# Narrow value products for three more heads, and a projection ahead of the last value piece, in a one-core decode step

## The chip, the cores and the metric

The kernel runs on one core of one Trainium2 chip. A time is the device time of one execution in microseconds (us). A core has a matrix engine (TensorE, PE in the profile, with its weight loads listed as PEld), a vector engine (VectorE, DVE), a scalar engine (ScalarE, ACT), GpSimd (POOL) and SyncE (SP), which here issues nearly all transfers. Each engine works through its own instructions in order and waits on semaphores for the others.

## The reference

A transformer block step for one token and a batch of four: a modulated layer norm, attention of 32 query heads over a cache of 8 key-value heads with 4096 positions each, and then a modulated MLP-Mixer whose token axis has length one.

```
mod = (silu(c) @ w_mod).reshape(4, 6, 1, 512)      # sa, ca, ga, sb, cb, gb
h = layernorm(x) * (1 + ca) + sa
q = (h @ wq)                       # 32 heads of 128
p = softmax(q k^T * 128**-0.5)     # each of 8 cached heads serves 4 query heads
x = x + ga * ((p v) @ wo)
h = layernorm(x) * (1 + cb) + sb
u = gelu(layernorm(h) * w1 + b1)   # for each channel, 1792 values
x = x + gb * (u @ w2 + b2)
```

All is float32. The key and value caches are 134 MB together.

## The kernel before

The cache is worked through in 32 "heads", one for each pair of batch entry and key-value head: head i belongs to batch entry i // 8. Each head's keys and values, 2 MB each, come through a ring of three large SBUF tiles (`ring`, tag "kv"). The transfers are issued by SyncE. For heads 0 to 23 a loop carries the work; heads 24 to 31 and the Mixer of the last two batch entries follow an order written out by hand in the string `PLAN` (lines 627 to 636), whose steps are read from left to right and issue their instructions at once. So each engine's order is the order in which the steps stand in that string.

The steps of a head i, with the letters of the plan:

- `s` scores (L238), `S`, `m`, `X`, `b`, `B`: the maximum; `e` exponentials (L268), with their sums; `t` transposes of the probabilities in two halves (L275).
- `l` (sums, L279): adds the sums up over partitions with a constant matrix, `grp`, or `grpl` for head 31. `L` (scale, L284 to L290): the reciprocal, spread into a selection tile of 4 x 4 columns, or of 4 for head 31 (L287).
- `v` (values): probabilities times values. For heads 0 to 30, eight products of 512 columns (L301), in two steps `vi.0` and `vi.1`: each takes four groups of positions at once and makes a 512-column result of which only the matching quarter is of use. For head 31, 32 products of 128 columns (`values_last`, L309), in four steps of 16, 8, 4 and 4 products. Either form writes 32 rows in one of four row groups of the result (`pv`, or `pve`) in turn.
- `V` (copy_v, L315): the result from PSUM to SBUF, 512 or 128 columns. `a` (pick, L324): one product for each 128 columns, four or one, which picks and normalises. `A` (copy_o, L329): its 128 x 4 result to SBUF.
- `p` (project): head times output weights. For heads up to 29, four products of 512 columns (L337) into `pa`, which `P` (add_up, L353) adds to the accumulator of its batch entry. For heads 30 and 31, 16 products of 128 columns each (L342), accumulated in `pgx`.

Around the end there are also `y` (the accumulator of the last batch entry folded, L358, into `pc`), `E` (the residual of the other heads from `pc`, L362 and L363), `I` (that residual added to `pgx` by a product, L685), `Y` (which names the tile `pgx` and issues nothing), `x` (two expansions for the Mixer of batch entry 2, L431), `f` (a gate multiplied into a piece of the output weights, L567) and `zs` (the first statistics of the last batch entry, L370). From there the last entry's norm and Mixer follow.

The last transfers, in the order in which SyncE issues them: values of head 28, of head 29, of head 30 in two halves, of head 31 in pieces of 16, 8, 4 and 4 groups of positions, and 1 MB of modulation weights. All of them have been issued by 353.5 us.

Where a value piece or a tile is used, the framework lets the engine wait for the transfer or for the last reader of its buffer.

Of the kernel before, what the change touches and what calls it, by code (L numbers as in the profile page):

```python
# [8 lines left out]
F32 = mybir.dt.float32  # L9
# [6 lines left out]
B, D, HQ, HKV, SK, DH, F = 4, 512, 32, 8, 4096, 128, 1792  # L16
# [3 lines left out]
P = 128  # L20
NS = B * HKV
NSM = 3 * NF + 16 + 1

# [8 lines left out]
def adaln_decode(ctx: ExitStack, tc: tile.TileContext, small, x, wmod, wq, kk, kv, vv, wo, out):  # L34
# [7 lines left out]
    ps_s = ctx.enter_context(tc.tile_pool(name="ps_s", bufs=2, space=PSUM))  # L42
    ps_v = ctx.enter_context(tc.tile_pool(name="ps_v", bufs=1, space=PSUM))
# [3 lines left out]
    mm = nc.tensor.matmul  # L47
    dv = nc.vector

    neg1 = pad.tile([1, 96], F32, name="neg1")[:, 0:1]  # L50
    sm = cst.tile([P, NSM], F32, name="sm")
    xr = wk.tile([P, D], F32, name="xr", tag="yw", bufs=1)[0:B]
# [28 lines left out]
    grp = cst.tile([P, 16, REP, 2], F32, name="grp")  # L81
    dv.tensor_copy(grp, eight.unsqueeze(1).unsqueeze(3).to_broadcast([P, 16, REP, 2]))
    grp = grp.rearrange("p j r e -> p (j r e)")
    grpl = cst.tile([P, 4, REP, 8], F32, name="grpl")
    dv.tensor_copy(grpl, eight.unsqueeze(1).unsqueeze(3).to_broadcast([P, 4, REP, 8]))
    grpl = grpl.rearrange("p c r x -> p (c r x)")
# [86 lines left out]
    def slots():  # L173
        return ring.tile([P, 2, SK], F32, name="kv", tag="kv")
# [29 lines left out]
    def load_wm5():  # L204
        t = slots().rearrange("p s (k n) -> p (s k) n", n=D)
        nc.sync.dma_start(t[:, 0:4], wmod[2][:, 1])
        WM[5] = t[:, 0:4]
        return t[:, 4:6]

    def load_key(t, i):  # L210
        nc.sync.dma_start(t, kv[i - 2][:, 0])
        key(t, i)

    def load_v(t, i, cuts):
        value(t, i)
        src = (kv[i][:, 1] if i < NS - 2 else vv[i - NS + 2]).rearrange("p (j d) -> p j d", d=DH)
        for lo, hi in zip(cuts, cuts[1:]):
            nc.sync.dma_start(VT[i][:, lo:hi], src[:, lo:hi])
# [12 lines left out]
    S, M, PL, SEL = {}, {}, {}, {}  # L231
# [38 lines left out]
    def turn(i, halves=range(2)):  # L270

        S.pop(i, None)
        for n in halves:
            p = PL[i][0][:, n * 512:(n + 1) * 512]
            dv.transpose(p, p)  # L275

    def sums(i):
        pl = ps_m.tile([P, 1], F32, name="pl", tag="m")
        mm(pl, grp if i < NS - 1 else grpl, PL[i][1], start=True, stop=True)  # L279
        SEL[i] = pl  # L280

    def scale(i):
        rl = wk.tile([P, 1], F32, name="rl")
        dv.reciprocal(rl, SEL[i])  # L284
        if i == NS - 1:
            SEL[i] = wk.tile([P, 1, REP], F32, name="sel", bufs=4)
            dv.tensor_scalar(SEL[i][:, 0], eight, rl, None, op0=OP.mult)  # L287
            return
        sel = wk.tile([P, 4, REP], F32, name="sel", bufs=4)
        dv.tensor_scalar(sel, sel4, rl, None, op0=OP.mult)  # L290
        SEL[i] = sel

    PV, PA = {}, {}

    def values(i, ks):
        if ks[0] == 0:
            PV[i] = ps_v.tile([P, 4 * DH], F32, name="pv", tag="pv")
        pT = PL[i][0]
        for k in ks:
            q = k % 4  # L300
            mm(PV[i][32 * q:32 * q + 32, :], pT[:, 128 * k:128 * k + 128:4],  # L301
               VT[i][:, 4 * k:4 * k + 4, :].rearrange("p j d -> p (j d)"), start=(k < 4), stop=(k >= 4))

    def values_last(i, ks, pv):
        PV[i] = pv
        pT = PL[i][0].rearrange("p (k r) -> p k r", r=32)
        for k in ks:
            for c in range(4):
                mm(pv[32 * c:32 * c + 32, :], pT[:, k * 4 + c, :], VT[i][:, k * 4 + c, :],  # L309
                   start=(k == 0), stop=(k == 7))  # L310
# [20 lines left out]
    def project(i, pa=None):  # L331
        b, h = divmod(i, HKV)
        oT = OT.pop(i)
        if pa is None:
            pa = ps_m.tile([P, D], F32, name="pa", tag="m")
            for g in range(REP):
                mm(pa[32 * g:32 * g + 32, :], oT[:, g:g + 1].to_broadcast([P, 32]), wo_t[h][:, g, :],  # L337
                   start=True, stop=True)
        else:
            for g in range(REP):  # L340
                for c in range(4):
                    mm(pa[32 * c:32 * c + 32, :], oT[:, g:g + 1].to_broadcast([P, 32]),  # L342
                       wo_t[h][:, g, c * P:(c + 1) * P], start=(g == 0 and h == HKV - 2),
                       stop=(g == REP - 1 and h == HKV - 1))
        PA[i] = pa
# [9 lines left out]
    def fold_groups(pool, acc, tag):  # L355
        pc = pool.tile([P, P], F32, name="pc", tag=tag)
        for c in range(4):
            mm(pc[32 * c:32 * c + 32, :], first, acc[:, c * P:(c + 1) * P], start=True, stop=True)  # L358
        return pc

    def residual(x1, pc):
        dv.tensor_mul(x1, pc, prep[:, 1])  # L362
        dv.tensor_add(x1, x1, prep[:, 0])  # L363
# [4 lines left out]
    def stats(xin, b):  # L368
        st = wk.tile([P, 6], F32, name="st")
        dv.bn_stats(st, xin)  # L370
        sm_ = wk.tile([P, 4, 6], F32, name="stm")
        dv.tensor_mul(sm_, st.unsqueeze(1).to_broadcast([P, 4, 6]), ident.rearrange("p (c r) -> p c r", c=4)[:, :, 8 * b:8 * b + 1].to_broadcast([P, 4, 6]))
        return sm_
# [190 lines left out]
    def fold_gate(gate, es):  # L564
        for e in es:
            w = wo_t[HKV - 2 + e // REP][:, e % REP]
            dv.tensor_mul(w, w, gate)  # L567
# [7 lines left out]
    for step in (turn, sums, scale):  # L575
        step(0)
    mix = None
    for i in range(NS - HKV):
# [7 lines left out]
        if i:  # L586
            pick(i - 1)
            copy_o(i - 1)
        turn(i + 1)
        sums(i + 1)  # L590
        scale(i + 1)
        if i:
            project(i - 1)
# [29 lines left out]
    pve = pgx = pc = ep = spare = slot = None  # L623
    gates = list(range(2 * REP))
    cuts = {NS - 1: (0, 16, 24, 28, 32), NS - 2: (0, 16, 32)}
    last = [(0, 1, 2, 3), (4, 5), (6,), (7,)]
# [4 lines left out]
    LK30 t27.1 S29 P26 v27.0 m29 l27 g LK31 T t28.1 X29 LT t28.0 s30 L27 S30 b29 v27.1 B29 e29 l28 m30 V27  # L631
    c LV28 L28 a27 g X30 t29.1 t29.0 l29 L29 s31 A27 LV29 b30 p27 x v28.0 B30 S31 m31 e30 f P27 LT LV30 X31
    v28.1 b31 l30 B31 e31 LV31 V28 L30 c t30.1 a28 l31 L31 v29.0 t31.1 v29.1 A28 p28 t30.0 V29 a29 v30.0
    A29 LW f v30.1 P28 p29 g V30 t31.0 a30 x v31.0 v31.1 v31.2 P29 A30 Y y f v31.3 p30 E V31 a31 I A31 p31
    zs g zq zg T2 c zx c zm zq zb0 zc T3 zg zb1 zw0 zn zw1
    """
    TABLE = {"s": scores, "S": row_max, "m": turn_max, "X": col_max, "b": spread_max, "B": copy_max, "e": expo,
# [6 lines left out]
    for step in PLAN.split():  # L644
        op, k = step.rstrip("0123456789."), step.lstrip("abcdefghijklmnopqrstuvwxyzABCDEFGHIJKLMNOPQRSTUVWXYZ")
        i, q = (int(n) for n in (k + ".0").split(".")[:2]) if k else (0, 0)
        if op in TABLE:
            TABLE[op](i)
        elif op in MIX:
            MIX[op]()  # L650
        elif op == "t":
            turn(i, [q])
        elif op == "v":
            if i < NS - 1:
                values(i, range(4 * q, 4 * q + 4))
                continue
            if q == 0:
                pve = ps_s.tile([P, 8, P], F32, name="pve", tag="s")[:, 0]
            values_last(i, last[q], pve)
        elif op == "p":  # L660
            project(i, pgx[:, 4] if i >= NS - 2 else None)
        elif op == "LT":
            slot = slots()
        elif op == "LK":
            load_key(slot[:, i % 2], i)
        elif op == "LV":
            load_v(slot[:, i % 2], i, cuts.get(i, (0, 32)))
        elif op == "LW":
            spare = load_wm5()
        elif op == "x":  # L670
            mix.expand(spare if mix.n == 6 else None)
        elif op == "f":
            fold_gate(gate, gates[:1])
            del gates[:1]
        elif step == "T":
            nc.scalar.activation(tab, neg1, AF.Exp)
        elif op == "Y":
            pgx = ps_s.tile([P, 8, P], F32, name="pgx", tag="s")
        elif op == "y":
            pc = fold_groups(ps_m, ACC.pop(B - 1), "m")  # L680
        elif op == "E":
            ep = cst.tile([P, P], F32, name="ep")
            residual(ep, pc)
        elif op == "I":
            mm(pgx[:, 4], ident, ep, start=False, stop=False)  # L685
        elif step == "T2":
            nc.scalar.activation(tab, neg1, AF.Abs_reciprocal_sqrt)
        elif step == "T3":
            nc.scalar.activation(tab, neg1, AF.Gelu_apprx_tanh)
        elif op == "zs":  # L690
            row.st = stats(pgx[:, 4], B - 1)
        elif op == "zx":
            dv.tensor_copy(XK[:, B - 1], pgx[:, 4])
        elif op == "zw":
            modmm(pgx[:, 0], 5, (0,) if i == 0 else (1, 2, 3))
        elif op == "zb":
            if i == 0:
                py = ps_s.tile([P, 8, P], F32, name="py3", tag="s")
            row.spread(py[:, 4:], (2 * i, 2 * i + 1))
# [35 lines left out]
```

## Time and profile before

| | |
|---|---|
| median of 3 runs | 389.47 us (389.02 to 390.22) |
| profiled execution, span | 386.9 us |
| mean granted clock of TensorE | 0.877 |
| read from memory | 157.32 MB, 407 GB/s over the span |
| TensorE busy | 298.9 us (77%) |
| VectorE busy | 215.2 us (56%) |
| chain that ended last | transfers 54%, TensorE 28%, VectorE 16% |

The profiled execution's own time is given by its span alone, from its first to its last instruction; the median of the runs is 2.57 us above the span. In a row of the timeline stand the start, the length of the merged group, the engine, the line, the operation, what it writes and reads, how often, and in square brackets how long the engine was idle before it and what ended that. A product of float32 counts as two records. Lengths of groups of products include a drain at the end that overlaps with what follows.

### The profile page before, as it was taken

To read this page: it belongs to the slowest core of one execution; us is meant where nothing else is said; L and a number is where in the kernel's file an instruction comes from. 1 tells how busy PE (TensorE), PEld (TensorE's weight loads), DVE (VectorE), ACT (ScalarE), POOL (GpSimd) and SP (SyncE) were. 2 spreads that over 40 slices of the span, in tenths; PEclk is the share of its full clock that TensorE was granted. 3 is DMA by queue.
4 is the path that set the end of the run, shared out by engine and by line. 5 is a ranking of instruction groups with operands and counts; after the bars stand their busy time and mean duration, and the time that the engine had idled before them with its cause. 6 is when DMAs were issued, how large, how long until landed. Compare 5 with 4: busy or idle time off the path is not lost.

```text
span 386.9 us, 5714 instructions
## 1 busy us (share of the span) xinstructions
PE 298.9 (77%) x2416; PEld 122.4 (32%) x2416; DVE 215.2 (56%) x516; ACT 108.0 (28%) x132; POOL 0.7 (0%) x6
## 2 busy tenths in 40 slices
PE   0765575863966949979888859999988887999984
PEld 0111121231323313334222323443323342444562
DVE  0420351620542524676766644676875579788766
ACT  0101120110110110113567210213783104757356
POOL 0000000000000000000000000000000000000000
PEclk9998875986695775989999985978999998899999
DMA  8999999999999999999999999999999999999910
GB/s 329 430 434 434 415 451 430 410 449 432 418 447 434 430 434 432 434 432 434 426 434 429 434 429 434 434 432 434 425 434 432 434 429 434 422 427 423 404 46 3
DMA packets 7281, 157.70 MB, mean 408 GB/s; under 512 B 964, under 2 KB 980, under 8 KB 1368
## 3 DMA queue, kind: packets, MB, share of 16 engines
q1 hardware_dynamic: 7248, 157.33, 94.8%
q8 instruction: 19, 0.31, 0.3%
q14 instruction: 6, 0.05, 0.0%
q10 hardware_dynamic: 8, 0.00, 0.0%
HBM read 157.32 MB, written 0.01 MB: 407 GB/s over the span
## 4 chain that ended last, share of the span: by engine, by line
DMA 54%; PE 28%; DVE 16%; issue 1%; SPq 1%; ACTq 0%; DVEq 0%
DMA kv<-in_kv 47%; PE s L238 8%; PE pv L301 7%; DMA wq<-in_wq 6%; DVE m L243 3%; DVE p L275 3%; PE pt L324 2%; PE pa L337 2%; PE pb L258 2%; DVE uu L431 1%; DVE mx L252 1%; DVE acc L353 1%; PE qs L152 1%; PE phb L417 1%; PE pve L309 1%
## 5 line engine op out<-in xcount | busy, mean ns | idle before, releaser
L238 PE MATMUL s<-kv,QT 128*32 128x512 f32 x512 | 76.2, 715 | 35.6 <-DMA kv<-in_kv 32.6
L268 ACT ACTIVATE p<-s,nm 128x1024 f32<-128x1024 f32 x32 | 35.6, 1114 | 199.0 <-DVE nm L263 198.9
L243 DVE TENSOR_REDUCE m<-s 128x1 f32<-128x1024 f32 x32 | 39.2, 1224 | 76.1 <-PE s L238 76.0
L301 PE MATMUL pv<-kv,p 128*32 128x512 f32 x496 | 75.0, 684 | 0.4 <-DMA kv<-in_kv 0.4
L275 DVE STREAM_TRANSPOSE p<-p 128x512 f32<-128x512 f32 x64 | 41.9, 687 | 1.7 <-ACT p L268 1.7
L324 PEld LDWEIGHTS pt<-sel,po 128*128 128x128 f32 x250 | 33.6, 208 | 28.7 <-issue 15.6
L238 PEld LDWEIGHTS s<-kv,QT 128*32 128x32 f32 x512 | 16.3, 125 | 81.3 <-DMA kv<-in_kv 45.3
L337 PE MATMUL pa<-wo,oT 128*32 128x512 f32 x240 | 35.3, 663 | 4.3 <-DVE oT L329 4.2
L324 PE MATMUL pt<-sel,po 128*128 128x4 f32 x250 | 36.2, 268 | 1.4 <-DVE po L315 1.4
L315 DVE COPY po<-pv 128x512 f32<-128x512 f32 x31 | 21.4, 689 | 17.0 <-PE pv L301 17.0
L252 DVE TENSOR_REDUCE mx<-pm 1x128 f32<-1x512 f32 x32 | 21.4, 671 | 0.8 <-PE pm L247 0.7
L258 PEld LDWEIGHTS pb<-neg,mx 1*128 1x128 f32 x64 | 10.8, 210 | 32.9 <-DVE mx L252 31.1
L487 ACT ACTIVATE u<-u 128x1024 f32<-128x1024 f32 x20 | 20.4, 1052 | 2.7 <-DVE u L431 2.6
L431 DVE TENSOR_SCALAR u<-hb,wr,sm 128x512 f32<-128x512 f32 x40 | 19.9, 541 | 1.0 <-PE py L442 0.9
L353 DVE TENSOR_TENSOR acc<-acc,pa 128x512 f32<-128x512 f32 x26 | 17.7, 681 | 3.6 <-PE pa L337 3.6
L268 ACT ACT_TABLE_LOAD x11 | 14.1, 1283 | 19.0 <-DVE nm L263 18.9
L137 PE MATMUL s<-wm,sT 128*4 128x512 f32 x16 | 8.4, 684 | 12.2 <-DVE sT L123 12.2
L258 PE MATMUL pb<-neg,mx 1*128 1x1 f32 x64 | 13.5, 278 | 5.3 <-DVE mx L252 5.3
L487 ACT ACT_TABLE_LOAD x13 | 16.7, 1283 | 0.2
L247 PE MATMUL pm<-ident,m 128*1 128x128 f32 x32 | 9.1, 286 | 9.8 <-DVE rl L284 3.8
L301 PEld LDWEIGHTS pv<-kv,p 128*32 128x32 f32 x496 | 14.1, 146 | 8.1 <-issue 2.1
L247 PEld LDWEIGHTS pm<-ident,m 128*1 128x1 f32 x32 | 2.5, 80 | 39.1 <-DVE rl L284 21.0
(144 smaller groups left out, 212.3 us busy)
## 6 DMA issues: line engine op xcount, KB each, us to landing
kv<-in_kv SPq DMA_DIRECT2D x28, 4096.0 KB, 20.8
wq<-in_wq SPq DMA_DIRECT2D x2, 4096.0 KB
wo<-in_wo SPq DMA_DIRECT2D x4, 2048.0 KB
kv<-in_kv SPq DMA_DIRECT2D x4, 2048.0 KB, 18.5
wm<-in_wmod SPq DMA_DIRECT2D x2, 2048.0 KB
kv<-in_kk SPq DMA_DIRECT2D x1, 4096.0 KB
kv<-in_vv SPq DMA_DIRECT2D x3, 1024.0 KB
wm<-in_wmod SPq DMA_DIRECT2D x1, 1024.0 KB
```

Of the source, the lines that this page charges most:

```text
L238: mm(s[32 * c:32 * c + 32, n * 512:(n + 1) * 512], QT[:, b, h, :], KT[i][:, (n * 4 + c) * 512:(n * 4 + c + 1) * 512], start=True, stop=True)
L243: dv.tensor_reduce(M[i], S[i], axis=AX.X, op=OP.max)
L252: dv.tensor_reduce(mx, M[i].rearrange("o (c r) -> o r c", c=4).unsqueeze(1).to_broadcast([1, 4, 32, 4]), axis=AX.X, op=OP.max)
L258: mm(pb, M[i].rearrange("o c r -> o (c r)"), neg1, start=True, stop=True)
L268: nc.scalar.activation(p, S[i], AF.Exp, bias=M.pop(i), accum_out=l)
L275: dv.transpose(p, p)
L301: mm(PV[i][32 * q:32 * q + 32, :], pT[:, 128 * k:128 * k + 128:4], VT[i][:, 4 * k:4 * k + 4, :].rearrange("p j d -> p (j d)"), start=(k < ...
L324: mm(pt, po[:, c * DH:(c + 1) * DH], sel[:, c, :], start=(c == 0), stop=(c == n - 1))
L337: mm(pa[32 * g:32 * g + 32, :], oT[:, g:g + 1].to_broadcast([P, 32]), wo_t[h][:, g, :], start=True, stop=True)
L353: dv.tensor_add(ACC[b], ACC[b], pa)
L431: dv.tensor_scalar(u[:, e, :], hb, wr[:, j:j + 1], b1[:, j:j + 1], op0=OP.mult, op1=OP.add)
L487: nc.scalar.activation(u, u, AF.Gelu_apprx_tanh)
```

## The change

Four things change.

1. Heads 28 to 30 form their value products as head 31 does: 32 products of 128 columns in place of 8 of 512. `values_last` becomes `values_narrow`, which takes its result tile from the pool of `pv` unless one is given.
2. Their sums and scales take the forms of head 31 (`grpl`, 4 columns), and since the result has 128 columns, the copy out of PSUM has 128 columns and the pick is one product.
3. The small copy of head 30's pick (`A30`) stands ahead of the expansions `x` rather than behind the addition `P29`; `P29` in turn falls behind the expansions and the gate product `f`.
4. The projection of head 30 (`p30`) and the residual of the other heads (`E`) stand ahead of the last value piece (`v31.3`) rather than behind it.

```diff
+NARROW = NS - 4
...
-        mm(pl, grp if i < NS - 1 else grpl, PL[i][1], start=True, stop=True)
+        mm(pl, grp if i < NARROW else grpl, PL[i][1], start=True, stop=True)
...
-        if i == NS - 1:
+        if i >= NARROW:
             SEL[i] = wk.tile([P, 1, REP], F32, name="sel", bufs=4)
...
-    def values_last(i, ks, pv):
-        PV[i] = pv
+    def values_narrow(i, ks, pv=None):
+        if ks[0] == 0:
+            PV[i] = ps_v.tile([P, DH], F32, name="pvn", tag="pv") if pv is None else pv
+        pv = PV[i]
         pT = PL[i][0].rearrange("p (k r) -> p k r", r=32)
         for k in ks:
             for c in range(4):
...
-    A29 LW f v30.1 P28 p29 g V30 t31.0 a30 x v31.0 v31.1 v31.2 P29 A30 Y y f v31.3 p30 E V31 a31 I A31 p31
+    A29 LW f v30.1 P28 p29 g V30 t31.0 a30 A30 x f v31.0 v31.1 v31.2 P29 Y y p30 E v31.3 V31 a31 I A31 p31
...
-            if i < NS - 1:
+            if i < NARROW:
                 values(i, range(4 * q, 4 * q + 4))
-                continue
-            if q == 0:
-                pve = ps_s.tile([P, 8, P], F32, name="pve", tag="s")[:, 0]
-            values_last(i, last[q], pve)
+            elif i < NS - 1:
+                values_narrow(i, range(4 * q, 4 * q + 4))
+            else:
+                if q == 0:
+                    pve = ps_s.tile([P, 8, P], F32, name="pve", tag="s")[:, 0]
+                values_narrow(i, last[q], pve)
```

## The prediction

> **What bounds the kernel now.** I read the page first, then the chain that ended last over the final sixty microseconds, then the timeline of that stretch, then the stretches of two microseconds for the granted clock. From the page:
>
> ```profile
> span 386.9 us, 5714 instructions
> DMA 54%; PE 28%; DVE 16%; issue 1%; SPq 1%; ACTq 0%; DVEq 0%
> q8 instruction: 19, 0.31, 0.3%
> ```
>
> The chain is transfers over most of the span. Its last part, in order of time (start, length, what):
>
> ```profile
> 336.33 21.56 DMA kv<-in_kv
> ...
> 358.03 1.95 PE pv L301 x16
> 359.98 0.86 PE pa L337 x8
> 360.84 1.00 PE pt L324 x8
> 361.84 2.04 PE pv L301 x16
> 363.88 0.86 PE pa L337 x8
> 364.74 1.01 PE pt L324 x8
> 365.75 1.78 PE pve L309 x56
> 367.53 0.22 PE pc L358 x8
> 367.75 0.42 PE pve L309 x8
> 368.17 0.87 PE pgx L342 x32
> 369.04 0.31 PE pt L324 x2
> 369.35 0.33 PE pgx L685 x2
> 369.68 1.05 PE pgx L342 x32
> ...
> 370.76 0.31 DVE st L370
> ```
>
> From 358.03, when head 29's values have landed, the chain is put down to TensorE alone, about 12.7 us of it up to the statistics at 370.76. Read only that far, every microsecond taken from the value products and picks of heads 29 and 30 would shorten the kernel. The timeline of the same stretch says otherwise:
>
> ```profile
> 361.77 2.11 PE L301 MATMUL pv<-kv,p 128*32 128x512 f32 x16
> 362.79 0.21 PEld L301 LDWEIGHTS pv<-kv,p 128*32 128x32 f32 x8 [0.80 <-DMA kv<-in_vv]
> 363.95 0.69 DVE L315 COPY po<-pv 128x512 f32<-128x512 f32 x1 [0.71 <-PE pv L301]
> 364.56 0.70 DVE L275 STREAM_TRANSPOSE p<-p 128x512 f32<-128x512 f32 x1
> 364.70 0.97 PEld L324 LDWEIGHTS pt<-sel,po 128*128 128x128 f32 x8 [0.86 <-DVE po L315]
> 365.18 0.96 DVE L431 TENSOR_SCALAR kv<-hb,wr,sm 128x512 f32<-128x512 f32 x2
> 365.68 1.85 PE L309 MATMUL pve<-kv,p 128*32 128x128 f32 x56
> 366.06 0.68 DVE L353 TENSOR_TENSOR acc<-acc,pa 128x512 f32<-128x512 f32 x1
> 366.66 0.15 DVE L329 COPY oT<-pt 128x4 f32<-128x4 f32 x1
> 366.73 0.68 DVE L567 TENSOR_TENSOR wo<-wo,gate 128x512 f32<-128x512 f32 x1
> 367.10 0.16 PEld L309 LDWEIGHTS pve<-kv,p 128*32 128x32 f32 x8 [0.17 <-DMA kv<-in_vv]
> 367.35 0.40 PE L358 MATMUL pc<-acc,g 128*32 128x128 f32 x8
> 367.74 0.16 PEld L309 LDWEIGHTS pve<-kv,p 128*32 128x32 f32 x8 [0.26 <-DMA kv<-in_vv]
> 368.35 0.28 DVE L315 COPY po<-pve 128x128 f32<-128x128 f32 x1
> 368.97 0.39 PE L324 MATMUL pt<-sel,po 128*128 128x4 f32 x2
> 369.39 0.16 DVE L329 COPY oT<-pt 128x4 f32<-128x4 f32 x1 [0.76 <-PE pt L324]
> ```
>
> Weight loads wait for transfers at 362.79 (second half of head 30), at 367.10 (third piece of head 31) and at 367.74 (its fourth and last). TensorE keeps pace with the stream; it does not lag behind it. The last piece can't be multiplied before about 367.74, whatever is saved ahead of it. **What sets the end is the time from there**: head 30's projection 0.87, a pick at 368.97, head 31's projection, the statistics and the last Mixer.
>
> **Narrow products of heads 28 to 30.** Eight products of 512 columns become 32 of 128 per head; in the records each counts twice, so 16 become 64. Head 31 shows the price: 56 of them in 1.85 us with a small wait inside, and the 32 of a projection, of the same shape, in 0.87. Two such are 1.74 for 64. The wide form takes 1.95 for 16 with its drain of about 0.2, so 1.75 issued. I take no change. Bounds: 0.3 less per head (the sixteen at 361.77 took 2.11, its wait included) to 0.4 more (56 in 1.85 scaled to 64 is 2.11, against 1.75). Cover: the next piece's landing.
>
> The copy out of PSUM falls from 0.69 to 0.28, the pick from 8 records (about 1.0) to 2 (0.31 in the chain): per head 0.4 on VectorE and 0.7 on TensorE, some 1.1 in a row, three times. The scale's output of 4 columns rather than 16, and the other constant in the sums, I cost at nothing: both stand ahead of the landing for which their head's pick waits anyway, and without that cover a product of this size is a part of the copy's 0.28.
>
> None of the 3.3 us reaches the end. For head 28 the next product waits for head 29's landing at 358.03. For head 29 the chain arrives at head 30 some 1.1 us sooner, at about 360.7, and its second half still waits until 362.79. For head 30 it reaches head 31 about 1.1 sooner than 365.68, where the first piece isn't in: 1.05 MB after 362.79, at the 157.70 MB in 386.9 us of the whole (408 GB/s), is an estimated 365.4. The 0.3 that may be gained there ends at 367.10, where the third piece lands. TensorE then idles where it used to catch up.
>
> **The order around the last piece.** On VectorE head 30's small copy (A30) goes ahead of the two expansions, and its addition for head 29 (P29) behind the gate product. On TensorE head 30's projection goes ahead of the last value piece. No transfer is moved and none is issued by a moved step; SyncE's, ScalarE's and GpSimd's orders stay.
>
> Walk it from the rows. Second half of head 30 at 362.79 as before; copy at 363.95 for 0.28, transpose to about 364.9. Head 29's projection issues until about 364.6; the pick with 0.39 is through at 365.0. VectorE waits about 0.1 for it, copies at 365.05, and takes 0.07 to the next start (366.66 to 366.73), 0.88 for the expansions (365.18 to 366.06), 0.60 for the product (366.06 to 366.66, the same length): P29 runs from about 366.6 to 367.3, half a microsecond later than before. The fold (pc) reads it. TensorE gets to the fold at 367.35 anyway, because of the third piece. So the later addition costs 0 to 0.1; I take 0. It has no slack left.
>
> From there, before against after. **Before:** fold, last piece at 367.74, projection hidden over the copy, pick at 368.97, that is 1.23 after the last piece. **After:** fold 367.35 with 0.22, projection 367.57 with 0.87, last piece at 368.44 instead of 367.74, its end with 0.42 at 368.86, then copy with 0.07 and 0.28 to 369.21, and 0.06 to the pick (as 364.64 to 364.70): 369.27. The projection filled TensorE while the copy ran; now the copy stands bare, and the piece that had landed at 367.74 waits 0.7 behind the projection. The gap between the third and the last landing, 0.64, is too small for 0.22 of piece, 0.22 of fold and 0.87 of projection. Pick to head 31's projection and all behind it keep their lengths: the residual (E, I) is ready before, since its two VectorE steps of 0.29 follow the fold by 0.9.
>
> The sum: 369.27 - 368.97 = **+0.3 us**. The profile's one execution has a span of 386.9 us; the median of the runs is 389.47, 2.57 above it for what lies around the span, and I keep that difference: 389.47 + 0.3 = **389.8**.
>
> **The rivals.**
>
> *Faster: the last piece lands late enough.* The new order needs 0.83 from the last piece to the pick (0.42, 0.07, 0.28, 0.06) where the old one needs 1.23. If TensorE had finished the projection when the piece lands, 0.4 would be gained: 389.1. It decides where the landing comes later than 367.74 by 0.3 to 0.4. The 0.26 of waiting at 367.74 speaks for a late piece, the projection's 0.87 against it. Chance 0.16. Even then the gain is inside 0.3% (1.17 us), which is about what a measurement of this kernel can tell from no change.
>
> *Slower: the instruction transfers.* Three heads issue 48 records and as many weight loads more each, less 6 of each for the picks: 252 instructions. The 19 instruction packets carry 0.31 MB, 16 KB each; 0.3% of 16 engines' 386.9 us is 18.6 us, about 1 us for each, on one transfer engine. An added packet, if it falls on the engine that ends last, delays the last pieces by up to 1.0: the third piece at 368.1, the pick at 370.2, so 1.2 over before: 390.7. For it: the engines are all but full until the end. Against it: one of sixteen must be the late one. Chance 0.2 for 0.5 or more of it.
>
> *Slower: the granted clock.* TensorE now idles in several pieces between 360.5 and 367. The stretches (length, busy time of each engine, clock, DMA share) show what a long idle piece does:
>
> ```profile
> 324.00:326.00 2.00, 0.36 (x1) 0.08 (x1) 2.00 (x4) 0.00 (x0) 0.00 (x0) 0.88 1.03 442
> 328.00:330.00 2.00, 2.00 (x24) 0.79 (x16) 0.34 (x1) 1.99 (x3) 0.00 (x0) 0.50 0.99 426
> ```
>
> After 0.36 us of work in 2 the clock was 0.50 at 328. If that happened here, the 3.4 us of TensorE's work between the fold and the statistics would double: about 393. Against it: even with 2 us taken out of the nine from 358 to 367, TensorE is busy over 70% of the time there. Chance 0.05. [...]
>
> *Slower: narrow products that don't overlap.* The view of line 309 gives the weight loads alone:
>
> ```profile
> L309 PEld LDWEIGHTS pve<-kv,p x64: 106/110/110, 365.7 to 367.8; 128*32 128x32 f32 x64
> ```
>
> If each of the 64 cost its own 0.11, a head would take 7.0 in place of 1.75. Head 29 from 358.03 to 365.1, projection and pick 1.2, head 30 to 373.3, 1.2 again: head 31 at 374.5 in place of 365.7, so about 398. The 56 in 1.85, 0.033 each, speak against it. Chance 0.02. [...]
>
> *The change does not reach the end at all:* 389.5, between forecast and the faster rival, in the likeliest one's range.
>
> **How the numbers follow.** Forecast (with the no-effect case) 0.57, late landing 0.16, instruction packets 0.20, clock 0.05, narrow products 0.02. The likeliest's own range is 389.3 to 390.2, its 0.3 plus or minus the spread of the runs before (389.02 to 390.22, 0.6 either side). Taking in the late landing below and most of the packets above gives 389.0 to 390.8. Over 0.3% slower (above 390.64) are the clock, the narrow products, and under half of the packets' case, with some of the forecast's upper tail: 0.20. Over 0.3% faster needs more than the 0.4 that any order here can give; 0.06 is left for what I don't see. Within: 0.74.
>
> **What would show it.** In the profile after: head 31's first products at about 365.4 behind a wait for a transfer; waits for transfers at all four pieces but the last; the last piece's products right behind the projection with no wait, near 368.4; the copy of head 31 with TensorE idle beside it; the pick near 369.3; the three copies at 0.28 and picks at 0.3 to 0.4. Wrong would be: a last piece still waiting for its transfer behind the projection (the gain then is 0.4), landings later than 367.74 by most of a microsecond, a clock under 1 after 360, or 64 narrow products over 2.1 us.

## The result, and the profile after

The changed kernel takes 390.18 us (median; 389.65 to 391.54) against 389.44 us (388.85 to 390.64) for the kernel before, measured in turn on the same chip. The ratio is 1.0017, with a 95% interval of 1.0009 to 1.0025: 0.35 to 0.97 us more, inside the 0.3% that was called no change.

The traced executions differ by more (1.4 us) than the medians (0.74), and this goes with it: the runs of the kernel before fall into two groups, 12 of 21 up to 389.5 us and 9 from 389.8 us on, the profiled one has the span of the lower group, all runs of the changed kernel but one lie between 389.65 and 390.66, and what sets the upper group no trace shows.

From the page of the changed kernel:

```profile
span 388.3 us, 5965 instructions
DMA 54%; PE 26%; DVE 16%; ACT 2%; issue 1%; SPq 0%; DVEq 0%; ACTq 0%
q8 instruction: 20, 0.33, 0.3%
```

The span is 1.4 us longer, there are 251 instructions more, and one instruction packet more. This execution took 390.09 us, 1.8 above its span. The chain of the changed kernel (start, length, what):

```profile
348.78 18.70 DMA kv<-in_vv
367.52 1.05 PE pve L312 x24
368.56 0.22 PE pc L361 x8
368.78 0.87 PE pgx L345 x32
369.66 0.26 PE pve L312 x8
369.94 0.30 DVE po L318
370.29 0.39 PE pt L327 x2
370.67 0.33 PE pgx L690 x2
371.00 1.05 PE pgx L345 x32
372.08 0.31 DVE st L373
```

Before, this chain ran through TensorE from 358.03. Now one transfer holds it until 367.5, the second piece of head 31's values, and only then do the pieces, the fold, the projection (0.87) and the last piece (0.26) follow. The copy at 369.94 now stands in the chain, which it did not before. The timeline of the same stretch:

```profile
358.17 1.95 PE L312 MATMUL pvn<-kv,p 128*32 128x128 f32 x64 [0.41 <-DMA kv<-in_kv]
360.19 0.29 DVE L318 COPY po<-pvn 128x128 f32<-128x128 f32 x1 [0.68 <-PE pvn L312]
360.92 0.39 PE L327 MATMUL pt<-sel,po 128*128 128x4 f32 x2
362.94 1.08 PE L312 MATMUL pvn<-kv,p 128*32 128x128 f32 x32 [0.62 <-DMA kv<-in_vv]
365.23 0.16 DVE L332 COPY oT<-pt 128x4 f32<-128x4 f32 x1 [0.23 <-PE pt L327]
365.60 1.00 DVE L434 TENSOR_SCALAR kv<-hb,wr,sm 128x512 f32<-128x512 f32 x2 [0.21 <-DMA kv<-in_vv]
366.38 2.18 PE L312 MATMUL pve<-kv,p 128*32 128x128 f32 x56 [1.19 <-DMA kv<-in_vv]
367.12 0.68 DVE L356 TENSOR_TENSOR acc<-acc,pa 128x512 f32<-128x512 f32 x1
368.14 0.16 PEld L312 LDWEIGHTS pve<-kv,p 128*32 128x32 f32 x8 [0.25 <-DMA kv<-in_vv]
368.38 0.40 PE L361 MATMUL pc<-acc,g 128*32 128x128 f32 x8
369.47 0.40 PE L312 MATMUL pve<-kv,p 128*32 128x128 f32 x8
370.29 0.39 PE L327 MATMUL pt<-sel,po 128*128 128x4 f32 x2 [0.41 <-DVE po L318]
372.08 0.30 DVE L373 BATCH_NORM_STATS2 st<-pgx 128x6 f32<-128x128 f32 x1 [1.20 <-PE pgx L345]
```

Set against the rows of before: head 29's products start at 358.17 rather than 358.03 and take the same 1.95; the copy and the pick have shrunk as meant; TensorE then idles, 0.62 and 1.19 in the waits for head 30's second half and for head 31's first piece. The third piece lands at 368.14 in place of 367.10. From there to head 31's pick it is 2.15 us, where it was 1.87. So of the 1.32 us by which the pick is later (370.29 against 368.97), 1.04 are a later landing and 0.28 are the order. Behind the pick nothing changed: the statistics are 1.32 later too.

What delayed the landing? The transfer queues between 360.5 and 367 us (packets, MB, share of 16 engines), changed kernel:

```profile
q1 hardware_dynamic: 628, 2.62, 98.1%
q8 instruction: 1, 0.02, 0.9%
```

and the kernel before in the same stretch, where this is the only queue that moved anything:

```profile
q1 hardware_dynamic: 650, 2.69, 100.2%
```

An instruction packet has moved into the last stretch. 0.9% of 16 engines over 6.5 us is 0.94 us of one engine's time; the trace has the packet from 364.08 to 365.01. The stream up to head 29 accounts for 0.14 of the 1.04, and a packet of 0.94 could account for the rest. Whether this pairing is a cause, the experiments had to tell.

### The profile page after: what moved, and what is told of

Read it like the earlier page. It is cut to its first block, busy times and chain, and to the rows that moved or that the text cites. A ratio compares the mean times of both kernels' runs of the same rounds, so it can differ in the third digit from the quotient of the medians.

```text
span 388.3 us, 5965 instructions
## 1 busy us (share of the span) xinstructions
PE 290.5 (75%) x2542; PEld 120.3 (31%) x2542; DVE 214.1 (55%) x516; ACT 108.0 (28%) x132; POOL 0.7 (0%) x6
## 4 chain that ended last, share of the span: by engine, by line
DMA 54%; PE 26%; DVE 16%; ACT 2%; issue 1%; SPq 0%; DVEq 0%; ACTq 0%
DMA kv<-in_kv 43%; PE s L239 10%; PE pv L302 5%; DMA kv<-in_vv 5%; DMA kv<-in_kk 4%; DVE m L244 4%; DVE p L276 3%; PE s L138 2%; DVE mx L253 2%; DMA sm<-in_small 2%; DVE acc L356 2%; PE pb L259 1%; PE pt L327 1%; PE pa L340 1%; PE py L439 1%
## 5 line engine op out<-in xcount | busy, mean ns | idle before, releaser
L302 PE MATMUL pv<-kv,p 128*32 128x512 f32 x448 | 64.0, 647 | 0.0
L327 PEld LDWEIGHTS pt<-sel,po 128*128 128x128 f32 x232 | 30.5, 204 | 28.1 <-issue 20.1
L340 PE MATMUL pa<-wo,oT 128*32 128x512 f32 x240 | 33.6, 632 | 4.2 <-DVE oT L332 4.2
L327 PE MATMUL pt<-sel,po 128*128 128x4 f32 x232 | 33.2, 265 | 1.2 <-DVE po L318 1.2
L318 DVE COPY po<-pv 128x512 f32<-128x512 f32 x28 | 19.3, 690 | 12.1 <-PE pv L302 12.1
L259 PEld LDWEIGHTS pb<-neg,mx 1*128 1x128 f32 x64 | 10.0, 194 | 30.9 <-DVE mx L253 29.2
L259 PE MATMUL pb<-neg,mx 1*128 1x1 f32 x64 | 12.7, 265 | 5.3 <-DVE mx L253 5.0
L302 PEld LDWEIGHTS pv<-kv,p 128*32 128x32 f32 x448 | 12.5, 146 | 5.0 <-issue 1.3
```

The costliest lines, as they stand in the source:

```text
L259: mm(pb, M[i].rearrange("o c r -> o (c r)"), neg1, start=True, stop=True)
L327: mm(pt, po[:, c * DH:(c + 1) * DH], sel[:, c, :], start=(c == 0), stop=(c == n - 1))
```

## Experiments

Three theories stood against each other: the **order** (the new plan costs, whatever the code's size), the **packets** (more instructions move the instruction packets to other places, whatever the instructions are), and the **narrow** products themselves. The medians of the kernel before beside the three groups of kernels were 389.57 (the first four), 389.19 (the next four) and 389.53 (the last four); ratios are against these.

**The order alone.** The kernel before with the new plan, wide products.

```diff
-... a30 x v31.0 v31.1 v31.2 P29 A30 Y y f v31.3 p30 E V31 a31 I A31 p31
+... a30 A30 x f v31.0 v31.1 v31.2 P29 Y y p30 E v31.3 V31 a31 I A31 p31
```

> The kernel before with the new order alone; the value products of heads 28 to 30 stay wide. If the order costs by itself (head 30's small copy waits for a wide pick ahead of the expansions, P29 falls behind, the fold and the projection stand ahead of the last piece): walked from the rows of before, head 30's small copy at 366.65, expansions to 367.7, the gate product to 368.3, P29 to 369.0, fold at 369.0, projection, last piece at 370.1, pick near 370.9 instead of 368.97, so about 1.9 us slower, near 391.3. If only the added instructions of the narrow products cost, the time stays within 0.3 us of before. The page keeps 19 instruction packets on queue 8 by either theory.

390.43 us (390.14 to 392.86), ratio 1.0019 (1.0001 to 1.0037). That is 0.86 above by the medians: the order costs, but less than half of the 1.9 that was expected. Its trace is of the longest of its executions, with a granted clock of 0.74 from 358 to 362 us, so its starts are not comparable; one wait in its timeline, where the clock is 1.00 again, is:

```profile
370.38 0.68 DVE L353 TENSOR_TENSOR acc<-acc,pa 128x512 f32<-128x512 f32 x1
371.12 0.42 PE L358 MATMUL pc<-acc,g 128*32 128x128 f32 x8 [1.00 <-DVE acc L353]
```

The fold waits a whole microsecond for P29. With wide products the larger pick and copy push A30, and P29 with it, still later. So the order costs through the addition that I had priced at nothing.

**The narrow products alone.** The changed kernel with the old plan.

```diff
-... a30 A30 x f v31.0 v31.1 v31.2 P29 Y y p30 E v31.3 V31 a31 I A31 p31
+... a30 x v31.0 v31.1 v31.2 P29 A30 Y y f v31.3 p30 E V31 a31 I A31 p31
```

> The changed kernel with the old order of the last steps; heads 28 to 30 stay narrow. If the added instruction packet makes the last pieces late (20 packets on queue 8, one of them between 364 and 367), the time stays 0.3 to 1.0 us above before, 389.8 to 390.4, and the third and fourth piece are waited for about 1 us later than at 367.10 and 367.74. If the order alone costs, the time returns to before, 389.4, or some 0.1 below. If the narrow products themselves are slow, 64 of them take over 2.1 us in the profile.

389.78 us (389.29 to 390.43), ratio 1.0002 (0.9987 to 1.0018). Its timeline:

```profile
368.20 0.16 PEld L312 LDWEIGHTS pve<-kv,p 128*32 128x32 f32 x8 [0.25 <-DMA kv<-in_vv]
368.82 0.16 PEld L312 LDWEIGHTS pve<-kv,p 128*32 128x32 f32 x8 [0.25 <-DMA kv<-in_vv]
370.05 0.39 PE L327 MATMUL pt<-sel,po 128*128 128x4 f32 x2
```

The third piece lands as late as in the changed kernel (368.20), with an instruction packet in the same stretch, so the late landing belongs to the narrow code and not to the order. From it to the pick it is 1.85 against 2.15: the order is worth 0.3, as the prediction walked it. The medians, from two measurements, point the same way: 390.18 less 389.78 is 0.4. The time alone does not show the late landing: the interval of the ratio lies on both sides of 1, and only the trace, against the trace of the kernel before, has the pick 1.08 later.

**The place of the packets alone.** A product near the start, at about 35 us (`px`, line 166 of the kernel before), is repeated: it writes the same result again. That moves every later instruction in the code and computes nothing new. Each repeat is 16 TensorE instructions; here eight, 128 in all, in the kernel before and in the changed one. That is about half a packet, by an estimate from the two traces: 2416 weight loads and 2416 products to 19 packets before, 2542 of each to 20 in the changed kernel, so 254 a packet, or 256 with TensorE's 30 waits and drains.

```diff
-    for c in range(4):
+    for c in list(range(4)) * 9:
```

> The kernel before with 32 more small products (128 more TensorE instructions) in the pause near 35 us, where TensorE waits 2.9 us for the first keys: they repeat the product px and change nothing. All later instruction packets then come half a packet of instructions earlier. If the place of the packets against the last pieces sets part of the end, the time moves: between -0.4 and +1.0 us, and the last pieces land at other times than 367.10 and 367.74. If packets do not matter, the time is that of before within 0.2 us.

> The changed kernel with the same 128 instructions near 35 us. If the packet between 364 and 367 delays the last pieces, it now falls near 361 and another near 368, and the time moves by up to 1 us, rather down than up: 389.4 to 390.2. If only order and products count, the time stays at 390.2 within 0.2.

The padded kernel before took 390.27 us (389.67 to 391.70), ratio 1.0008 (0.9991 to 1.0025), which does not settle it; the padded changed kernel 390.87 (390.41 to 391.72), ratio 1.0024 (1.0009 to 1.0038). The latter is a miss by either theory, 389.4 to 390.2 for the packets and 390.0 to 390.4 without them: its packet moved to 362.00 us, which is still in the stretch, and the third piece still landed at 368.20. Both traces show something else besides. In two fences each, the stretch from 358 to 362 (length, busy time of each engine, clock, DMA share, GB/s) and the timeline of head 31, first the padded kernel before:

```profile
358.00:362.00 4.00, 3.81 (x23) 1.50 (x26) 1.82 (x6) 1.96 (x2) 0.00 (x0) 0.60 1.00 423
```

```profile
367.60 1.74 PE L309 MATMUL pve<-kv,p 128*32 128x128 f32 x56
```

and the padded changed kernel:

```profile
358.00:362.00 4.00, 3.83 (x68) 3.36 (x72) 1.86 (x6) 1.78 (x2) 0.00 (x0) 0.57 1.01 424
```

```profile
366.45 2.18 PE L312 MATMUL pve<-kv,p 128*32 128x128 f32 x56
369.00 0.42 PE L361 MATMUL pc<-acc,g 128*32 128x128 f32 x8 [0.37 <-DVE acc L356]
370.93 0.39 PE L327 MATMUL pt<-sel,po 128*128 128x4 f32 x2 [0.41 <-DVE po L318]
```

Both were granted little over half the clock in the same 4 us. With wide products TensorE comes to head 31 at 367.60, 1.92 later than in the trace before, and the pick (370.58) is 1.61 later. With narrow ones it comes at 366.45, where it is in the changed kernel anyway; the fold then waits 0.37 for P29, and the pick is 0.64 later than in the changed kernel. So the microseconds that the narrow form saves are real, and in this pair of traces they take up most of a halved clock. Without one they end as idle time.

**Narrow for head 30 only, three orders.** With one narrow head in place of three (84 instructions more than before in place of 251), the packet should stay out of the last stretch. The third order brings head 30's projection between the pieces, where TensorE idles anyway. The old order is that of the kernel before, the new one that of the changed kernel; the early one is in the diff.

```diff
-NARROW = NS - 4
+NARROW = NS - 2
...
+... a30 A30 x v31.0 Y p30 v31.1 P29 y v31.2 f E v31.3 V31 a31 I A31 p31
```

> Narrow products for head 30 alone (and 31, as always), old order. 84 TensorE instructions more instead of 252. If the added instruction packet is what makes the last pieces late, there is no third packet between 354 and 367 here: third and fourth piece at 367.1 and 367.7 as before, and the time is 388.9 to 389.4, at or below before, since TensorE's lag ahead of head 31 is gone. If narrow products cost by themselves, a third of what the kernel with all three shows against before, with the pieces at their places.

> The same with the new order of the last steps. By the walk of the prediction the order alone costs 0.3 where the last piece is on time: 0.3 to 0.4 above the same kernel with the old order, 389.3 to 389.7. If the order cost only because the pieces were late, the two are equal.

> Narrow for head 30 alone, and its projection not between the third and the last piece but between the first and the second, where TensorE waits for transfers; the fold ahead of the third piece; the residual ahead of the last. From the landings 365.2, 366.4, 367.1 and 367.7: projection done by 366.95, last piece at 367.8, copy at 368.3 to 368.6, pick at 368.65 to 368.8 instead of 368.97. 0.2 to 0.4 below the same kernel with the old order, 388.7 to 389.1. If the projection's place does not matter, equal to it.

390.15 us (389.78 to 390.98), 390.03 (389.73 to 391.33) and 390.15 (389.72 to 391.62); ratios 1.0020, 1.0020 and 1.0025, with intervals that begin at 1.0004 or above. No packet lies between 360.5 and 367 in any of the three, and the third piece lands at 367.57 and 367.24 in the first two (masked by TensorE in the third). The picks come at 369.44, 369.78 and 369.12: the new order's later and the early order's sooner than the old one's, as expected. All the same the times are equal, and 0.8 to 1.0 above the kernel before, where 388.9 to 389.4, 389.3 to 389.7 and 388.7 to 389.1 had been expected: three misses, which neither the order nor the landing explains. The old order's timeline shows where the time went:

```profile
367.57 0.16 PEld L312 LDWEIGHTS pve<-kv,p 128*32 128x32 f32 x8 [0.26 <-DMA kv<-in_vv]
370.08 1.06 PE L345 MATMUL pgx<-wo,oT 128*32 128x128 f32 x26
371.60 0.42 PE L345 MATMUL pgx<-wo,oT 128*32 128x128 f32 x6 [0.46 <-issue]
372.08 0.30 DVE L373 BATCH_NORM_STATS2 st<-pgx 128x6 f32<-128x128 f32 x1 [2.06 <-PE pgx L345]
```

Head 31's projection stops after 26 of 32 records, with nothing to wait for that the profile shows; in the early order it stops at the same place for 0.57. In the new order the stop is shorter, but the 32 records still take 1.32 in place of 1.08. The statistics start at 372.08, 371.80 and 371.87, against 370.76 before. A sooner pick only makes the pause longer. And where the pieces land in time, the new order's addition is late, as this timeline of the new order shows:

```profile
367.12 0.68 DVE L356 TENSOR_TENSOR acc<-acc,pa 128x512 f32<-128x512 f32 x1
367.86 0.42 PE L361 MATMUL pc<-acc,g 128*32 128x128 f32 x8 [0.19 <-DVE acc L356]
370.43 1.32 PE L345 MATMUL pgx<-wo,oT 128*32 128x128 f32 x32
```

Third piece to pick is 2.54 there (367.24 to 369.78) against 1.87 in the old order: the order costs 0.67, of which 0.28 is the bare copy and the rest P29.

**The early order with three narrow heads.**

```diff
-... a30 A30 x f v31.0 v31.1 v31.2 P29 Y y p30 E v31.3 V31 a31 I A31 p31
+... a30 A30 x v31.0 Y p30 v31.1 P29 y v31.2 f E v31.3 V31 a31 I A31 p31
```

> The same early projection with heads 28 to 30 narrow, that is 168 more TensorE instructions than the kernel with head 30 alone and nothing else. If the packet that they bring makes the pieces late: third piece at about 368.1, and 0.5 to 1.0 above the kernel with head 30 alone. If the number of instructions does not matter: equal within 0.2.

389.86 us (388.99 to 390.53), ratio 1.0007 (0.9993 to 1.0021). A miss: it was to be 0.5 to 1.0 above the one with head 30 alone and lies 0.3 below. It pays for the late landing (the packet is back, the first piece starts at 366.69 behind 1.34 of waiting, the pick at 370.23) and has no pause in head 31's projection (statistics at 372.02); the other pays for the pause and not for the landing. Against the changed kernel's 390.18, from another measurement, the early order is 0.3 shorter, which the spread of the runs does not settle.

**The pause in the kernel before.** If the pause comes from the place of the code, 80 added TensorE instructions should put it into the unchanged kernel, at the same instruction.

```diff
-    for c in range(4):
+    for c in list(range(4)) * 6:
```

> The kernel before, with 80 more TensorE instructions in the pause near 35 us, so that every later instruction packet is needed 80 instructions earlier. With head 30 narrow alone (84 instructions more) TensorE paused 0.5 us inside head 31's projection, after 26 of its 32 records, with no wait in the profile, and the kernel was 0.2% slower. If that pause is a packet that comes too late and has nothing to do with head 30's products, it shows up here at the same place, and the time is 0.4 to 1.0 above before: 389.7 to 390.3. If it came from the narrow products, there is no pause here and the time is that of before within 0.2.

390.09 us (389.70 to 391.70), ratio 1.0014 (0.9999 to 1.0029). Its timeline:

```profile
367.27 0.16 PEld L309 LDWEIGHTS pve<-kv,p 128*32 128x32 f32 x8 [0.16 <-DMA kv<-in_vv]
369.14 0.39 PE L324 MATMUL pt<-sel,po 128*128 128x4 f32 x2
369.78 1.07 PE L342 MATMUL pgx<-wo,oT 128*32 128x128 f32 x28
371.30 0.41 PE L342 MATMUL pgx<-wo,oT 128*32 128x128 f32 x4 [0.45 <-issue]
371.75 0.30 DVE L370 BATCH_NORM_STATS2 st<-pgx 128x6 f32<-128x128 f32 x1 [2.03 <-PE pgx L342]
```

There it is, after 28 of 32. The third piece is only 0.17 later than without the padding, but from the pick to the statistics it is 2.61 us in place of 1.79. Between 369 and 371.5 its transfers hold one instruction packet of 2.3% of 16 engines, 0.9 us (369.11 to 370.04). That alone does not mark the pause, for the kernel before has such a packet there too (369.44 to 370.36) and no pause. What marks it is the place in the code. Counting TensorE's instructions (weight loads, products and its few waits) in the order in which they start, the one after the stop is the 4546th here and in head 30 alone in the old and the early order, and it starts 1.25 to 1.41 us after the packet's transfer has ended. The shorter stop of the new order is ahead of the 4546th too. In the kernel before the 4546th starts only at 372.67, 2.31 after it. The unchanged work with its code 80 instructions further on takes 0.56 more by the medians, three quarters of what the whole change costs. The interval of the ratio just takes in 1, but none of the 12 executions is under 389.70, where 18 of the 35 unpadded ones beside it are.

**Moving the pause away.** Narrow head 30 with 176 instructions of padding in the old and the early order, and with 112 in the early one, which should put the pause near the fold and the third piece of head 31 (there the 12 of the diff is an 8). With the 84 of the narrow head the 176 make 260, by the estimate above about one packet.

```diff
-    for c in range(4):
+    for c in list(range(4)) * 12:
```

> Head 30 narrow alone, old order, with 176 more instructions near 35 us: together with its own 84 that is 260, so that the packets are needed where the kernel before needs them, within 4 instructions. If the packets' place is what made head 30 alone slower: no pause in head 31's projection, and the time falls from 0.2% above before to before or 0.2 below, 389.0 to 389.4. If narrow products are to blame, it stays at 0.2% above.

> The same with head 30's projection between the first and the second value piece. If the packets are out of the way, the pick comes 0.2 to 0.3 sooner than with the old order: 388.7 to 389.2, the one that could beat the kernel before. A packet may now be needed inside the early projection itself, where it would cost up to 0.7; then 389.5 to 390.

> The same with 112 in place of 176 instructions: by the count from the pause, the packet is needed near the fold and the third piece, and the next one in the last Mixer's gate products, which nothing waits for. Between 388.7 and 389.8 by whether TensorE waits for a transfer there anyway. If the place of the packets does not matter, the two with early projection are equal.

390.04 us (389.85 to 391.37), 390.39 (388.99 to 393.08) and 390.17 (389.35 to 392.27); ratios 1.0015, 1.0020 and 1.0016, none with an interval clear of 1. The old order is the useful pair, since it differs from the unpadded one by the padding alone. Its queues between 360.5 and 367 us, and then its timeline:

```profile
q8 instruction: 1, 0.02, 0.9%
```

```profile
368.39 0.16 PEld L312 LDWEIGHTS pve<-kv,p 128*32 128x32 f32 x8 [0.25 <-DMA kv<-in_vv]
370.88 1.08 PE L345 MATMUL pgx<-wo,oT 128*32 128x128 f32 x32
```

The pause is gone (32 records in one run), and a packet is now in that stretch, with the third piece at 368.39 in place of 367.57 and the pick at 370.24 in place of 369.44. The time did not fall to the expected 389.0 to 389.4. This half of the expectation was missed, and the miss is what shows the packets as a cause: padding alone changes a pause into a late landing. With 112 the pause stands close to where it was put, two records before the end of the second piece and ahead of the fold, and again the 4546th instruction is the one after it, 1.25 us behind a packet; but that trace too has the clock at 0.57 from 358 to 362, and the 176 of the early order 0.81, so these two say nothing about the end. The pause with 112, in that kernel's timeline:

```profile
368.34 0.61 PE L312 MATMUL pve<-kv,p 128*32 128x128 f32 x14
369.39 0.30 PE L312 MATMUL pve<-kv,p 128*32 128x128 f32 x1 [0.44 <-issue]
```

Over all kernels whose third piece can be read: with a packet between 360.5 and 367 it lands at 368.14 (the change), 368.20, 368.20 and 368.39; without one at 367.10 (before), 367.24, 367.27 and 367.57. No version had a median below that of the kernel before, in whose trace the packets happen to lie where nobody waits for them.

## Why the prediction was right or wrong

390.18 lies in the range and in the likeliest case's own range, and "within 0.3%" came true. The forecast of +0.3 us stands against a ratio that gives +0.35 to +0.97, and against +1.32 in the traces. The largest step that failed is the landing of the third piece, which the sum kept at 367.10: it came 1.04 later, and landings late by most of a microsecond are one of the signs of being wrong that the prediction names. The order, the only term of its sum, gave 0.28 of the 0.3.

- *None of the 3.3 us reaches the end.* Right. The copies (0.29) and the pick (0.39) shrank, the products' 64 records took the same 1.95 as the wide sixteen, and the gain ended as 0.62 and 1.19 of idle time ahead of the transfers.
- *Narrow products cost nothing.* Right in length. Wrong that they cost nothing at all: their price lies in where the longer code puts the instruction packets, not in the engine.
- *The order, from the fold: 1.92 to the pick.* Right: 368.38 to 370.29 is 1.91. The last piece stands behind the projection with no wait, and the copy stands bare. The rival of a late last piece did not come in.
- *P29: "the later addition costs 0 to 0.1; I take 0".* This step failed too, without a price here. It ends at 367.80, not 367.3: VectorE's copy A30 is at 365.23 rather than 365.05, and the expansions start only at 365.60, where 0.07 was allowed. In the changed kernel this is hidden, since the third piece is later still. Where the pieces land in time (head 30 alone in the new order), it costs 0.4 (0.67 in all for the order), and with wide products the fold waited 1.00.
- *First piece at an estimated 365.4.* It started at 366.38 behind a transfer. The mean rate was not the mistake: without a packet in the stretch the first piece started behind its transfer at 365.46 and 365.79 (head 30 alone, new and old order), with one at 366.38 and 366.69 (three heads, new and early order).
- *The instruction packets, given 0.20.* This rival is what the trace shows, on top of the order: it said third piece 368.1 and pick 370.2, measured 368.14 and 370.29. Its time, 390.7, was too high by 0.5, for the reason given under the median below. "One of sixteen must be the late one" was a poor argument against it: in each of the four kernels above with a packet in that stretch, the landing was late.
- *The clock, given 0.05.* Not in the changed kernel's trace, which has 1.00 in each 2 us from 358 to 368. But the stretch to fear was 358 to 362 (0.57 to 0.81 in five of the runs above), not the idle piece behind it. That idleness lowers it is the author's reading of one stretch (0.36 us of work in 324 to 326, 0.50 at 328); in the five runs TensorE was busy for 3.48 to 4.00 of the 4 us ahead of 358.
- *Median = span + 2.57.* The step that kept the total near the truth by luck. The changed kernel's profiled execution is 1.8 above its span; the rest of the 2.57 was that the profiled execution of the kernel before was shorter than its median. Hence +1.32 in the traces and about +0.7 in the medians.

## What to carry to other kernels

Where the end is bound by transfers, an engine's saving can end as idle time in front of the next landing, as 0.62 and 1.19 us did here: read the wait brackets beside the chain before crediting it. An edit that adds instructions can also move the instruction packets, as 251 more put one at 364.08 here, where none had been; before a difference of a few tenths of a per cent is put down to the edit, run the unchanged kernel with its code shifted by a harmless padding, which here moved its median by 0.56 us where 0.74 were in question. When a small step is moved to the front of an engine's queue, walk everything that it pushes back with the measured gaps, not with the shortest gap seen elsewhere.

## What the runs showed of the hardware that was not expected

- *One instruction packet near the bound end went with a landing later by about its own length.* It took 0.93 us (364.08 to 365.01 in the changed kernel), and the third piece was 0.8 to 1.1 us later with it than without. 251 added instructions brought one more packet (19 to 20), as did 260 in the padded old order; 80 and 84 did not. The packets, 0.31 MB in 19, carry 16 KB each, and the estimated 254 to 256 instructions to a packet fit these counts. That the packet fell on a transfer engine that ends last is inferred from the late landings, since the traces name no engine; why it did so each time stays open.
- *TensorE paused in the middle of a run of products.* The same projection stopped for 0.45 to 0.57 us after 26 or 28 of 32 records, with no wait that the profile shows, and with the padding it moved to another product, always ahead of TensorE's 4546th instruction. That it waits for its own instructions fits this, and the packet whose transfer ended 1.25 to 1.41 us before it went on. But that transfer had ended 0.8 to 0.95 us before the stop began, so what fills the time between stays open.
- *The clock was granted at 0.57 to 0.81 from 358 to 362 us in some executions* of the padded and reordered kernels, and with it the last pick came 1.61 us later in the wide form, 0.64 in the narrow one.
